# Decode attention beside a gated unit: output weights at the end of the load stream, values in 512-column products, softmax steps between transposes

## The chip, the cores and the metric

The kernel runs on one core of a Trainium2 chip. A core has TensorE (PE in the profile; its weight loads are the row PEld), VectorE (DVE), ScalarE (ACT), GpSimd (POOL), SyncE (SP) and 16 DMA engines that move data between the device memory and SBUF. TensorE writes its results to PSUM, eight banks of 128 partitions by 512 floats. The metric is the device time of one execution in microseconds (us).

## The reference

Two batch rows, one new token each, hidden size 512. The token is normalised, goes through attention over the last 4096 keys of a cache with 8 key/value heads (32 query heads, four to each kv head, head size 128), and in parallel through a gated unit with 1792 hidden columns; the input and both results are added. Everything is float32.

```python
# B, D = 2, 512; Hq, Hkv, Sk, Dh = 32, 8, 32768, 128; F = 1792
W = min(4096, max(256, Sk // 4))                        # 4096
q = (xn @ wq).reshape(B, 1, Hq, Dh).transpose(0, 2, 1, 3)
k = repeat(k_cache[:, :, Sk - W:, :], Hq // Hkv, axis=1)
v = repeat(v_cache[:, :, Sk - W:, :], Hq // Hkv, axis=1)
p = softmax(einsum("bhqd,bhkd->bhqk", q, k) * Dh ** -0.5)
a = einsum("bhqk,bhkd->bhqd", p, v).transpose(0, 2, 1, 3).reshape(B, 1, Hq * Dh) @ wo
gate, up = xn @ W_gate, xn @ W_up
h = gate * (gate > 0) * up
out = x + a + h @ W_down                                # xn = layernorm(x)
```

The inputs are 95 MB, of which the used part of both caches is 67 MB (32 heads of 2 MB: K and V, two batch rows, eight kv heads), wq and wo 8 MB each, and the three gated-unit weights 11 MB.

## The kernel before

**Loads.** All large loads go out on SP's queue, in the order in which the program uses the data: wq in four, w_gate and w_up in two each, w_down in two, then the caches head by head, then wo. They share a ring of eight buffers (`load`, line 66). A load waits until the buffer eight loads earlier has been read. x comes on ACT's queue: once on 32 partitions (`x32`, line 98, for the layer norm) and, in four small loads, spread over 128 partitions (`x4`, line 100, for the residual).

**Start.** The layer norm runs on 32 partitions; its transpose `xnT` is the stationary operand of the q, gate and up products. q is spread with zeros into `qz` (line 191), so that one product of 32 stationary columns fills the rows of one head and leaves the others unchanged. The gated unit ends in `hT`; its product with w_down (lines 226 and 227, `project`) starts the sum of the output in the PSUM tile `y_ps`.

**Attention.** The work is in four groups g = (r, b): four kv heads c of one half r of the heads, for one batch row b. For each head, `transposes` (line 234) turns 4096 x 128 keys in 32 TensorE transposes, four to a PSUM tile `pk` of 512 columns; there are four such PSUM buffers, and ACT and DVE take turns in copying them to `kT`. `scores` (line 245) multiplies `kT` with `qz` in eight products of 512 columns; four of them run on different 32-column tiles of TensorE. The scores of a whole group collect in one PSUM tile `s`: its 128 rows are (quarter of the keys q, head c, half s1, query i), its columns 512 keys.

`softmax` (line 257) is one chain over TensorE, DVE and ACT: row maxima (`m`), their transpose (`mt`), the maximum per query (`mx`, `mb`), spread back over the rows (`nm_ps`, `nm`), exponential with row sums on ACT (`p`, `l`), the transpose of the probabilities (`pp`, `pt`), and the sums per query (`lp`, `rl`). `values` (line 292) takes 32 products per head with 128 columns of V each and 4 stationary columns of `pt`, into four row quarters of `o_ps`. `finish` (line 303) copies `o_ps` once per group and, in 64 products of one column each, adds the quarters and turns the result (`op`); a multiplication with `rl` puts it into `oT`.

**Order.** The order on every engine is that of the program text (`manual_schedule`, line 63). The loop at line 329 takes, for each head c of group g, the key head of g (`kwork`: its transposes, then the scores of the head before) and the value head of g - 1. Before the first value head of a group stands the whole softmax of g - 1, after the last its `finish`. After the loop come the last softmax, the first quarter of wo, the last four value heads, the last `finish`, and the rest of wo. The projection with wo adds to `y_ps`, four products per 128 rows of wo in column tiles; the residual `x4` is added by DVE at the end (line 360), and 4 KB are stored.

Of the kernel before, what the change touches and what calls it, by code (L numbers as in the profile page):

```python
# [20 lines left out]
def kernel(  # L21
# [13 lines left out]
    P = 128  # L35
# [9 lines left out]
    # Four 128x32 column tiles of the PE run side by side: one quarter of the keys in each.  # L45
# [63 lines left out]
    # Of slot n = (c, s1), columns 32n..32n+31 hold q at 4n..4n+3 and zeros elsewhere.  # L109
# [7 lines left out]
    o_ps = ps_1.tile([P, C, P], F32, name="o_ps")  # L117
    nc.vector.memset(o_ps, 0.0)
    y_ps = ps_1.tile([P, P], F32, name="y_ps")
    nc.vector.memset(y_ps, 0.0)  # L120
# [3 lines left out]
    oT = const.tile([P, HKV, REP, B, 16], F32, name="oT")  # L124
    nc.gpsimd.memset(oT, 0.0)

    # Score rows are (q, c, s1, i): selections of them, from the identity.
    by_c = const.tile([P, C], F32, name="by_c")
    nc.vector.tensor_reduce(
        out=by_c, in_=ident.rearrange("p (q c w) -> p c q w", q=Q, c=C), op=ALU.add, axis=AX.XY  # L130
    )
    by_i = const.tile([P, REP], F32, name="by_i")
    nc.vector.tensor_reduce(
        out=by_i, in_=ident.rearrange("p (n i) -> p i n", i=REP), op=ALU.add, axis=AX.X
    )
    same_i = const.tile([P, REP, DD], F32, name="same_i")
    nc.vector.tensor_copy(same_i, by_i[:, :, None].to_broadcast([P, REP, DD]))
    sel_i = const.tile([P, REP], F32, name="sel_i")
    nc.vector.tensor_reduce(
        out=sel_i, in_=ident.rearrange("p (q w) -> p w q", q=Q)[:, 0:REP, :], op=ALU.add, axis=AX.X  # L140
    )

# [11 lines left out]
    # one Newton step on the square root: 1 / sqrt(v) = 2 / (v / s + s)  # L154
# [49 lines left out]
    dw = [load_down(h) for h in range(2)]  # L204
# [15 lines left out]
    def project(lhsT, w, start, stop):  # L220
        for e in range(Q):
            nc.tensor.matmul(  # L222
                y_ps[32 * e:32 * e + 17, :], lhsT.rearrange("p b s -> p (b s)")[:, 0:17], w[:, e * P:(e + 1) * P], start=start, stop=stop
            )

    for k in range(FB):
        project(hT[:, k], dw[k // 7][:, k % 7], k == 0, False)

# [1 line left out]
    # oT[(i, dd), kv, j, b]: head 4 kv + i, column 4 dd + j  # L230
    kts, ss, pts, rls = {}, {}, {}, {}
    turn = [0]

    def transposes(g, c, kt_in):
        kt = ktp.tile([P, W], F32, name=f"kT{g}_{c}", tag="kT")
        kts[g, c] = kt
        for s in range(W // 512):
            pk = ps_kt.tile([P, 512], F32, name=f"pk{g}_{c}_{s}", tag="kt")
            for u in range(4):
                j = 4 * s + u  # L240
                nc.tensor.transpose(pk[:, u * P:(u + 1) * P], kt_in[:, j * P:(j + 1) * P], ident)  # L241
            (nc.vector.tensor_copy if turn[0] % 2 else nc.scalar.copy)(kt[:, s * 512:(s + 1) * 512], pk)  # L242
            turn[0] += 1

    def scores(g, c):
        if c == 0:
            ss[g] = ps_1.tile([P, 512], F32, name=f"s{g}", tag="s")
        for s1 in range(S1):
            n = c * S1 + s1
            for q in range(Q):  # L250
                lo = (q * S1 + s1) * 512
                nc.tensor.matmul(  # L252
                    ss[g][32 * q:32 * q + 32, :], qz[:, g, 32 * n:32 * n + 32],
                    kts[g, c][:, lo:lo + 512], start=(n == 0), stop=(n == NSLOT - 1),
                )

    def softmax(g):
        m = work.tile([P, 1], F32, name=f"m{g}", tag="m")
        nc.vector.tensor_reduce(out=m, in_=ss[g], op=ALU.max, axis=AX.X)  # L259
        mt = ps_1.tile([1, P], F32, name=f"mt{g}", tag="misc")  # L260
# [8 lines left out]
        )  # L269
        nm_ps = ps_1.tile([P, 1], F32, name=f"nm_ps{g}", tag="misc")  # L270
# [8 lines left out]
        nc.scalar.activation(p, ss[g], AF.Exp, bias=nm, scale=SCALE, accum_out=l)  # L279
        pp = ps_1.tile([P, 4, P], F32, name=f"pp{g}", tag="misc")  # L280
        for u in range(4):
            nc.tensor.transpose(pp[:, u], p[:, u * P:(u + 1) * P], ident)  # L282
        pts[g] = work.tile([P, 4, P], F32, name=f"pt{g}", tag="pt")
        nc.vector.tensor_copy(pts[g], pp)  # L284
        lc = work.tile([P, C], F32, name=f"lc{g}", tag="lc")
        nc.vector.tensor_scalar(lc, by_c, l, None, op0=ALU.mult)
        lp = ps_1.tile([P, C], F32, name=f"lp{g}", tag="misc")
        nc.tensor.matmul(lp, same_i.rearrange("p i d -> p (i d)"), lc, start=True, stop=True)  # L288
        rls[g] = work.tile([P, C], F32, name=f"rl{g}", tag="rl")
        nc.vector.reciprocal(rls[g], lp)  # L290

    def values(g, c, v):
        for s1 in range(S1):
            for u in range(4):
                for q in range(Q):
                    lo = 32 * q + REP * (c * S1 + s1)
                    j = 4 * (q * S1 + s1) + u
                    nc.tensor.matmul(  # L298
                        o_ps[32 * q:32 * q + REP, c, :], pts[g][:, u, lo:lo + REP], v[:, j * P:(j + 1) * P],
                        start=(s1 == 0 and u == 0), stop=(s1 == S1 - 1 and u == 3),  # L300
                    )

    def finish(g):
        r, b = divmod(g, B)
        on = work.tile([P, C, P], F32, name=f"on{g}", tag="on")
        nc.scalar.copy(on, o_ps)  # L306
        ov = on.rearrange("p c (d j) -> p c j d", j=REP)
        op = ps_1.tile([P, C, REP], F32, name=f"op{g}", tag="misc")
        for c in range(C):
            for j in range(REP):  # L310
                for i in range(REP):
                    nc.tensor.matmul(  # L312
                        op[32 * i:32 * i + 32, c, j:j + 1], ov[:, c, j], sel_i[:, i:i + 1], start=True, stop=True
                    )
        nc.vector.tensor_tensor(  # L315
            oT[:, r * C:(r + 1) * C, :, b, 0], rls[g][:, :, None].to_broadcast([P, C, REP]), op, op=ALU.mult
        )
# [3 lines left out]
    def kwork(g, c, kt_in):  # L321
        transposes(g, c, kt_in)
        if pend:
            scores(*pend.pop())
        pend.append((g, c))
# [3 lines left out]
    for g in range(1, NG):  # L329
        for c in range(C):  # L330
            kt_in = load_kv(k_cache, "k", g, c)
            v_in = load_kv(v_cache, "v", g - 1, c)
            kwork(g, c, kt_in)
            if c == 0:
                softmax(g - 1)
            values(g - 1, c, v_in)
        finish(g - 1)
    scores(*pend.pop())
    g = NG - 1
    softmax(g)  # L340
    wt = load_wo(0, 2)
    vin = [load_kv(v_cache, "v", g, c) for c in range(C)]

    def project_wo(kv0, n, wt):
        for v in range(n):
            for j in range(REP):
                project(oT[:, kv0 + v, j], wt[:, v, j * D:(j + 1) * D], False, False)

    project_wo(0, 2, wt)
    for c in range(C):  # L350
        values(g, c, vin[c])
    finish(g)
    for kv in (2, 4):
        project_wo(kv, 2, load_wo(kv, 2))
    for kv, j0, j1 in ((6, 0, 4), (7, 0, 3), (7, 3, 4)):
# [34 lines left out]
```

## Time and profile before

| | us |
|---|---|
| median of 3 runs | 242.74 |
| lowest, highest | 241.59, 243.03 |
| span of the profiled execution | 239.9 |
| PE busy | 183.5 (76%) |
| PE weight loads busy | 130.7 (54%) |
| DVE busy | 62.6 (26%) |
| ACT busy | 46.9 (20%) |
| SP queue's loads, as a share of 16 DMA engines | 93.8% |

The profiled execution's own time is known by its span, from its first instruction to its last; the median of the runs is 2.84 us above that. The page divides the busy time by engine and by line. An f32 product of TensorE is recorded as two matmul records and a transpose as one, so that the 32 value products of a head stand as 64 records. The granted clock is the share of full speed that TensorE had; its mean is 0.885. The view of stages gives, for stretches of the span, the busy time of each engine with its number of instructions in brackets, the clock, the busy share of the DMA engines and the GB/s that they moved. The chain of waits follows the work that ended last back to the start: each row has its start, its length, the engine and the tile; "issue" is time in which the engine waited for nothing that the profile shows.

### The profile page before, as it was taken

What the parts mean: (1) busy time and instruction counts of PE and PEld (TensorE: products, weight loads), DVE (VectorE), ACT (ScalarE), POOL (GpSimd) and SP (SyncE); (2) the same over time, 40 slices, a digit from 0 to 9 for tenths busy, and PEclk for the clock granted to TensorE, in tenths of its full rate; (3) what the DMA queues carried; (4) which work ended last, traced back from release to release, by engine and by line L of the source; (5) the groups of instructions that cost most, each with busy time, mean ns of one, the idle gap of its engine ahead of it and who ended that gap; (6) DMA issues with size and microseconds to landing.
All of it is one profiled execution on the core that took longest, in us unless ns stands there. A gap on an engine that the chain in (4) does not pass through costs nothing.

```text
span 239.9 us, 6378 instructions
## 1 busy us (share of the span) xinstructions
PE 183.5 (76%) x2984; PEld 130.7 (54%) x2984; DVE 62.6 (26%) x122; ACT 46.9 (20%) x81; POOL 3.0 (1%) x9
## 2 busy tenths in 40 slices
PE   0194656685799949999594999989499998589464
PEld 0020111365666638777581777777277776269364
DVE  4400101102644433224043134404313440210000
ACT  2000000002433613223031123313112330100000
POOL 5000000000000000000000000000000000000000
PEclk9999788979999997999778599997769998759869
DMA  6999999999999999999999999999999999999700
GB/s 235 416 411 399 405 407 434 436 429 426 429 432 432 429 427 426 426 437 429 429 423 429 429 427 434 432 426 426 432 426 426 425 440 423 422 423 425 322 22 3
DMA packets 8030, 95.44 MB, mean 398 GB/s; under 512 B 796, under 2 KB 932, under 8 KB 2244
## 3 DMA queue, kind: packets, MB, share of 16 engines
q1 hardware_dynamic: 7820, 94.90, 93.8%
q8 instruction: 23, 0.38, 0.6%
q10 hardware_dynamic: 184, 0.13, 0.2%
q14 instruction: 3, 0.02, 0.0%
HBM read 95.03 MB, written 0.00 MB: 396 GB/s over the span
## 4 chain that ended last, share of the span: by engine, by line
PE 65%; DMA 24%; issue 4%; DVE 4%; ACT 2%; ACTq 0%
PE pk L241 25%; PE o_ps L298 14%; PE s L252 13%; DMA k<-in_A_k_cache_dram 10%; DMA wg<-in_B_W_gate_dram 7%; DMA x<-in_A_x_dram 7%; PE y_ps L222 4%; PE op L312 4%; PE pp L282 2%; ACT p L279 1%; PE g_ps L199 1%; DVE m L259 1%; DVE pt L284 1%; ACT on L306 1%; PE lp L288 1%
## 5 line engine op out<-in xcount | busy, mean ns | idle before, releaser
L241 PE MATMUL pk<-ident,k 128*128 128x128 f32 x512 | 64.8, 289 | 4.3 <-DMA k<-in_A_k_cache_dram 4.3
L241 PEld LDWEIGHTS pk<-ident,k 128*128 128x128 f32 x512 | 60.8, 150 | 10.2 <-issue 6.8
L242 DVE COPY kT<-pk 128x512 f32<-128x512 f32 x64 | 44.3, 692 | 69.9 <-PE pk L241 69.1
L242 ACT COPY kT<-pk 128x512 f32<-128x512 f32 x64 | 37.5, 586 | 97.6 <-PE pk L241 97.6
L298 PE MATMUL o_ps<-v,pt 128*4 128x128 f32 x1024 | 35.6, 299 | 2.3 <-issue 2.3
L298 PEld LDWEIGHTS o_ps<-v,pt 128*4 128x4 f32 x1024 | 29.0, 94 | 11.3 <-issue 8.2
L252 PE MATMUL s<-kT,qz 128*32 128x512 f32 x256 | 32.1, 619 | 0.0
L175 PE MATMUL q_ps<-wq,xnT 128*32 128x512 f32 x64 | 11.6, 878 | 4.9 <-DMA wq<-in_A_wq_dram 4.5
L312 PE MATMUL op<-sel_i,on 128*32 128x1 f32 x512 | 9.2, 199 | 7.2 <-issue 4.4
L252 PEld LDWEIGHTS s<-kT,qz 128*32 128x32 f32 x256 | 7.2, 112 | 12.6 <-issue 12.6
L312 PEld LDWEIGHTS op<-sel_i,on 128*32 128x32 f32 x512 | 8.6, 155 | 8.6 <-issue 4.6
L315 DVE TENSOR_TENSOR oT<-rl,op 128x16 f32<-128x16 f32 x4 | 0.7, 183 | 38.5 <-PE op L312 38.5
L222 PE MATMUL y_ps<-wo,oT 128*17 128x128 f32 x256 | 10.3, 335 | 0.0
L175 PEld LDWEIGHTS q_ps<-wq,xnT 128*32 128x32 f32 x64 | 2.4, 151 | 12.7 <-DMA wq<-in_A_wq_dram 6.4
L222 PEld LDWEIGHTS y_ps<-wo,oT 128*17 128x17 f32 x256 | 9.0, 120 | 0.6
L165 PE MATMUL xt_ps<-ident,xn 32*128 32x32 f32 x4 | 0.6, 287 | 11.3 <-DVE xn L162 11.3
L306 ACT COPY on<-o_ps 128x512 f32<-128x512 f32 x4 | 2.3, 585 | 26.7 <-PE o_ps L298 26.7
L282 PE MATMUL pp<-ident,p 128*128 128x128 f32 x16 | 3.6, 363 | 4.3 <-ACT p L279 4.3
L199 PE MATMUL g_ps<-wg,xnT 128*32 128x448 f32 x32 | 4.9, 749 | 2.5 <-DMA wg<-in_B_W_gate_dram 2.5
L165 PEld LDWEIGHTS xt_ps<-ident,xn 32*128 32x128 f32 x4 | 0.5, 208 | 11.2 <-issue 11.2
L279 ACT ACTIVATE p<-s,nm 128x512 f32<-128x512 f32 x4 | 2.7, 687 | 18.7 <-DVE nm L276 18.7
L199 PE MATMUL u_ps<-wu,xnT 128*32 128x448 f32 x32 | 3.4, 544 | 3.8 <-DMA wu<-in_B_W_up_dram 3.8
(60 smaller groups left out, 53.7 us busy)
## 6 DMA issues: line engine op xcount, KB each, us to landing
k<-in_A_k_cache_dram SPq DMA_DIRECT2D x16, 2048.0 KB, 29.7
v<-in_A_v_cache_dram SPq DMA_DIRECT2D x16, 2048.0 KB, 29.8
wq<-in_A_wq_dram SPq DMA_DIRECT2D x4, 2048.0 KB, 14.7
wo<-in_A_wo_dram SPq DMA_DIRECT2D x3, 2048.0 KB, 28.1
wg<-in_B_W_gate_dram SPq DMA_DIRECT2D x2, 1792.0 KB, 20.9
wu<-in_B_W_up_dram SPq DMA_DIRECT2D x2, 1792.0 KB
wd<-in_B_W_down_dram SPq DMA_DIRECT2D x2, 1792.0 KB, 15.2
wo<-in_A_wo_dram SPq DMA_DIRECT2D x1, 1024.0 KB
```

The source lines that it names most:

```text
L175: nc.tensor.matmul(q_ps[r][32 * c:32 * c + 32, :], xnT[:, kc, :], wqt[kc][:, n * 512:(n + 1) * 512], start=(kc == 0), stop=(kc == KC - 1),)
L199: nc.tensor.matmul(dst[32 * c:32 * c + 32, :], xnT[:, kc, :], wt[kc // 2][:, kc % 2, c * FQ:(c + 1) * FQ], start=(kc == 0), stop=(kc == KC ...
L222: nc.tensor.matmul(y_ps[32 * e:32 * e + 17, :], lhsT.rearrange("p b s -> p (b s)")[:, 0:17], w[:, e * P:(e + 1) * P], start=start, stop=stop)
L241: nc.tensor.transpose(pk[:, u * P:(u + 1) * P], kt_in[:, j * P:(j + 1) * P], ident)
L242: (nc.vector.tensor_copy if turn[0] % 2 else nc.scalar.copy)(kt[:, s * 512:(s + 1) * 512], pk)
L252: nc.tensor.matmul(ss[g][32 * q:32 * q + 32, :], qz[:, g, 32 * n:32 * n + 32], kts[g, c][:, lo:lo + 512], start=(n == 0), stop=(n == NSLOT ...
L259: nc.vector.tensor_reduce(out=m, in_=ss[g], op=ALU.max, axis=AX.X)
L279: nc.scalar.activation(p, ss[g], AF.Exp, bias=nm, scale=SCALE, accum_out=l)
L282: nc.tensor.transpose(pp[:, u], p[:, u * P:(u + 1) * P], ident)
L298: nc.tensor.matmul(o_ps[32 * q:32 * q + REP, c, :], pts[g][:, u, lo:lo + REP], v[:, j * P:(j + 1) * P], start=(s1 == 0 and u == 0), stop=( ...
L306: nc.scalar.copy(on, o_ps)
L312: nc.tensor.matmul(op[32 * i:32 * i + 32, c, j:j + 1], ov[:, c, j], sel_i[:, i:i + 1], start=True, stop=True)
```

## The change

- w_down's two loads and their projection move from before the caches to behind the last value loads; all of wo comes after them, in seven loads of 16, 16, 16, 8, 4, 2 and 2 KB per partition (before: six loads of 2, 2, 2, 1, 0.75 and 0.25 MB, the first ahead of the last value heads). The layout of wo changes with it: partition p holds 16 consecutive rows of one half (`load_wo(r, j0, j1)`).
- `values` takes 8 products per head with 512 columns of V and 16 stationary columns (four key columns u by four queries i). Of a result's 16 x 512 entries only those where u fits the column block count. ACT or DVE copies it, and `gather` picks and adds the right blocks with a stationary selection `pick`: four products of 128 columns per head, into one PSUM tile `oa` for the whole group. `finish` is a DVE multiplication; `spread_heads` brings the rows of two groups into `oT` with eight products, once per half.
- `softmax` is a generator. In the loop its steps stand between the `pk` tiles of the next group's first key head; `kT` is kept in halves of 2048 keys (three buffers instead of two full ones). The last group's softmax has no transposes beside it.
- `pk` has three PSUM buffers instead of four; `o_ps` has two tiles.
- The four loads of `x4` are gone; x is added by four products of `x32` with a selection `xsel`, which start the sum in `y_ps`.

The selections (`pick`, `by_h`, `spread`, `xsel`) are built from the identity on GpSimd and DVE ahead of the layer norm, in place of `by_c`, `by_i`, `same_i` and `sel_i`.

In the program order of TensorE, at the start of a group (here the second), before: the last transposes of key head 0, the scores of the head before it, the steps of the softmax, the first value head.

```order
L241 MATMUL pk_0_7_636<-ident,k_0_589 128x128 x4
L252 MATMUL s_462<-kT_3_532,qz 32x512 x8
L261 MATMUL mt_652<-ident,m_650 1x128
L272 MATMUL nm_ps_658<-ones,mb_656 32x1 x4
L282 MATMUL pp_668<-ident,p_665 128x128 x4
L288 MATMUL lp_677<-lc_675,same_i 128x4
L298 MATMUL o_ps<-v_0_591,pt_673 4x128 x32
```

The same place on TensorE now, from the second `pk` tile of key head 0 on:

```order
L241 MATMUL pk_0_0_1_562<-ident,k_0_545 128x128 x4
L262 MATMUL mt_568<-ident,m_560 1x128
L241 MATMUL pk_0_0_2_574<-ident,k_0_545 128x128 x4
L274 MATMUL nm_ps_580<-ones,mb_572 32x1 x4
L241 MATMUL pk_0_0_3_590<-ident,k_0_545 128x128 x4
L241 MATMUL pk_0_1_0_597<-ident,k_0_545 128x128 x4
L286 MATMUL pp_603<-ident,p_587 128x128 x4
L241 MATMUL pk_0_1_1_610<-ident,k_0_545 128x128 x4
L294 MATMUL lp_616<-l_588,by_h 16x1
L241 MATMUL pk_0_1_2_620<-ident,k_0_545 128x128 x4
L251 MATMUL s_632<-kT_0_0_553,qz 32x512 x4
L306 MATMUL o_ps_99<-v_0_547,pt_608 16x512 x8
```

One to two `pk` tiles stand between any two steps of the softmax, and the value head has 8 products instead of 32 (a second `pk` tile ahead of the scores is left out).

In the order of SP's queue, the end of the load stream before, from the last value load of the loop on:

```order
L68 DMA v_3_1846<-in_A_v_cache_dram 128x4096
L68 DMA wo_2044<-in_A_wo_dram 128x2x2048
L68 DMA v_0_2046<-in_A_v_cache_dram 128x4096
L68 DMA v_1_2048<-in_A_v_cache_dram 128x4096
L68 DMA v_2_2050<-in_A_v_cache_dram 128x4096
L68 DMA v_3_2052<-in_A_v_cache_dram 128x4096
L68 DMA wo_2282<-in_A_wo_dram 128x2x2048
L68 DMA wo_2316<-in_A_wo_dram 128x2x2048
L68 DMA wo_0_2350<-in_A_wo_dram 128x2048
L68 DMA wo_0_2368<-in_A_wo_dram 128x1536
L68 DMA wo_3_2382<-in_A_wo_dram 128x512
L361 DMA out_dram<-yo 4x2x128
```

and now, from the last group's third value load on:

```order
L69 DMA v_2_1573<-in_A_v_cache_dram 128x4096
L69 DMA v_3_1575<-in_A_v_cache_dram 128x4096
L69 DMA wd_1577<-in_B_W_down_dram 128x3584
L69 DMA wd_1579<-in_B_W_down_dram 128x3584
L69 DMA wo_0_1740<-in_A_wo_dram 128x4096
L69 DMA wo_8_1774<-in_A_wo_dram 128x4096
L69 DMA wo_0_1808<-in_A_wo_dram 128x4096
L69 DMA wo_8_1842<-in_A_wo_dram 128x2048
L69 DMA wo_12_1860<-in_A_wo_dram 128x1024
L69 DMA wo_14_1870<-in_A_wo_dram 128x512
L69 DMA wo_15_1876<-in_A_wo_dram 128x512
L416 DMA out_dram<-yo 4x2x128
```

Nine loads now stand behind the last cached value head, where there were five.

The diff, cut to its core:

```diff
-    ktp = ctx.enter_context(tc.tile_pool(name="ktp", bufs=2))
+    ktp = ctx.enter_context(tc.tile_pool(name="ktp", bufs=3))
-    ps_kt = ctx.enter_context(tc.tile_pool(name="ps_kt", bufs=4, space=PSUM))
+    ps_kt = ctx.enter_context(tc.tile_pool(name="ps_kt", bufs=3, space=PSUM))
+    ps_s = ctx.enter_context(tc.tile_pool(name="ps_s", bufs=1, space=PSUM))
...
+    def load_wo(r, j0, j1):
+        rows = NJ * P
+        src = wo[r * rows:(r + 1) * rows, :].rearrange("(p j) e -> p j e", p=P)[:, j0:j1, :]
+        return load(f"wo{r}_{j0}", src, [P, j1 - j0, D])
...
-    x4 = const.tile([P, P], F32, name="x4")
-    for e in range(Q):
-        nc.scalar.dma_start(
-            x4[32 * e:32 * e + 32, :],
-            bass.AP(tensor=x.tensor, offset=x.offset + e * P, ap=[[D, B], [0, 16], [1, P]]),
-        )
...
+    o_ps = [ps_1.tile([P, 512], F32, name=f"o_ps{k}") for k in range(2)]
...
-    dw = [load_down(h) for h in range(2)]
...
-    for k in range(FB):
-        project(hT[:, k], dw[k // 7][:, k % 7], k == 0, False)
...
+    def transposes(g, c, s1, kt_in):
+        kt = ktp.tile([P, HW], F32, name=f"kT{g}_{c}_{s1}", tag="kT")
+        kts[g, c, s1] = kt
+        for q in range(Q):
+            pk = ps_kt.tile([P, 512], F32, name=f"pk{g}_{c}_{s1}_{q}", tag="kt")
+            for u in range(4):
+                j = 4 * (4 * s1 + q) + u
+                nc.tensor.transpose(pk[:, u * P:(u + 1) * P], kt_in[:, j * P:(j + 1) * P], ident)
+            evacuate(kt[:, q * 512:(q + 1) * 512], pk)
+            yield
...
     def values(g, c, v):
+        o = o_ps[c % 2]
         for s1 in range(S1):
-            for u in range(4):
-                for q in range(Q):
-                    lo = 32 * q + REP * (c * S1 + s1)
-                    j = 4 * (q * S1 + s1) + u
-                    nc.tensor.matmul(
-                        o_ps[32 * q:32 * q + REP, c, :], pts[g][:, u, lo:lo + REP], v[:, j * P:(j + 1) * P],
-                        start=(s1 == 0 and u == 0), stop=(s1 == S1 - 1 and u == 3),
-                    )
+            for q in range(Q):
+                n = (q * C + c) * S1 + s1
+                lo = (4 * s1 + q) * 512
+                nc.tensor.matmul(
+                    o[32 * q:32 * q + 16, :], pts[g][:, n].rearrange("p u i -> p (u i)"), v[:, lo:lo + 512],
+                    start=(s1 == 0), stop=(s1 == S1 - 1),
+                )
+        ons[c] = work.tile([P, 4, P], F32, name=f"on{g}_{c}", tag="on")
+        evacuate(ons[c].rearrange("p u d -> p (u d)"), o)
...
+    def gather(g, c):
+        if c == 0:
+            oa[g] = ps_1.tile([HR, P], F32, name=f"oa{g}", tag="oa")
+        for u in range(4):
+            nc.tensor.matmul(
+                oa[g], pick[:, u, 12 - 4 * c:28 - 4 * c], ons[c][:, u],
+                start=(c == 0 and u == 0), stop=(c == C - 1 and u == 3),
+            )
...
+        nc.vector.tensor_scalar(osb[r][:, b], oa[g], rls[g], None, op0=ALU.mult)
...
+    def kwork(g, c, kt_in, others=()):
+        others = list(others)
+        for s1 in range(S1):
+            for _ in transposes(g, c, s1, kt_in):
+                if others and next(others[0], "end") == "end":
+                    others.pop(0)
+            if pend:
+                scores(*pend.pop())
+            pend.append((g, c, s1))
...
-            kwork(g, c, kt_in)
             if c == 0:
-                softmax(g - 1)
+                scores(*pend.pop())
+                kwork(g, c, kt_in, [softmax(g - 1)])
+            else:
+                kwork(g, c, kt_in)
+                gather(g - 1, c - 1)
             values(g - 1, c, v_in)
+            if c == 0 and g > 1:
+                finish_r = g - 2
+                if finish_r % B == B - 1:
+                    spread_heads(finish_r // B)
+        gather(g - 1, C - 1)
         finish(g - 1)
...
+    vin = [load_kv(v_cache, "v", g, c) for c in range(C)]
+    dw = [load_down(h) for h in range(2)]
+    for _ in softmax(g):
+        pass
...
+    for c in range(C):
+        values(g, c, vin[c])
+        if c:
+            gather(g, c - 1)
+    gather(g, C - 1)
+    finish(g)
+    for k in range(FB):
+        project(hT[:, k], dw[k // 7][:, k % 7], False)
+    spread_heads(R - 1)
+    half = NJ // 2
+    for r, j0, j1 in ((0, 0, half), (0, half, NJ), (1, 0, half), (1, half, half + 4), (1, half + 4, NJ - 2),
+                      (1, NJ - 2, NJ - 1), (1, NJ - 1, NJ)):
+        wt = load_wo(r, j0, j1)
+        for j in range(j0, j1):
+            project(oT[:, r, j], wt[:, j - j0], (r, j) == (R - 1, NJ - 1))
...
-    nc.vector.tensor_tensor(yo, x4, y_ps, op=ALU.add)
+    nc.vector.tensor_copy(yo, y_ps)
```

More of the change, by code (lines that the diff above doesn't have):

```diff
@@ L218, with evacuate @@
     nc.vector.tensor_copy(hT[:, :, :, 0], ht_ps)
-    def project(lhsT, w, start, stop):
-        for e in range(Q):
+    HW = W // S1
+    ss, pts, rls = {}, {}, {}
+    kts, osb = {}, {}
+    turn = [0]
+    def evacuate(dst, src):
+        (nc.vector.tensor_copy if turn[0] % 2 else nc.scalar.copy)(dst, src)
+        turn[0] += 1
+    def transposes(g, c, s1, kt_in):
[8 more added lines that the diff above has]
+            yield
@@ L222, in project, with scores @@
+    def scores(g, c, s1):
+        if (c, s1) == (0, 0):
+            ss[g] = ps_s.tile([P, 512], F32, name=f"s{g}", tag="s")
+        n = c * S1 + s1
+        kt = kts.pop((g, c, s1))
+        for q in range(Q):
             nc.tensor.matmul(
-                y_ps[32 * e:32 * e + 17, :], lhsT.rearrange("p b s -> p (b s)")[:, 0:17], w[:, e * P:(e + 1) * P], start=start, stop=stop
-            )
-    for k in range(FB):
-        project(hT[:, k], dw[k // 7][:, k % 7], k == 0, False)
-    kts, ss, pts, rls = {}, {}, {}, {}
@@ L232 @@
[L232 to L238, printed above, removed]
-            for u in range(4):
[L240 to L249, printed above, removed]
-            for q in range(Q):
[L251 to L255, printed above, removed]
+                ss[g][32 * q:32 * q + 32, :], qz[:, g, 32 * n:32 * n + 32],
@@ L257, in softmax @@
+                kt[:, q * 512:(q + 1) * 512], start=(n == 0), stop=(n == NSLOT - 1),
+            )
     def softmax(g):
@@ L282, in softmax @@
             nc.tensor.transpose(pp[:, u], p[:, u * P:(u + 1) * P], ident)
[L283 to L289, printed above, removed]
+        pts[g] = work.tile([P, Q * NSLOT, 4, REP], F32, name=f"pt{g}", tag="pt")
@@ L303, in finish @@
+    oa = {}
+    def gather(g, c):
[5 more added lines that the diff above has]
+                start=(c == 0 and u == 0), stop=(c == C - 1 and u == 3),
+            )
     def finish(g):
         r, b = divmod(g, B)
-        on = work.tile([P, C, P], F32, name=f"on{g}", tag="on")
-        nc.scalar.copy(on, o_ps)
-        ov = on.rearrange("p c (d j) -> p c j d", j=REP)
@@ L308, in finish @@
[L308 to L317, printed above, removed]
@@ L319, with spread_heads @@
-    pend = []
[L321 to L325, printed above, removed]
+        if b == 0:
+            osb[r] = const.tile([HR, B, P], F32, name=f"osb{r}")
+        nc.vector.tensor_scalar(osb[r][:, b], oa[g], rls[g], None, op0=ALU.mult)
+    def spread_heads(r):
+        op = ps_1.tile([P, NJ, B], F32, name=f"op{r}", tag="misc")
+        for e in range(NE):
+            nc.tensor.matmul(
+                op, spread[:, e].rearrange("h k e -> h (k e)"),
+                osb[r][:, :, e * NJ:(e + 1) * NJ].rearrange("h b j -> h j b"),
+                start=(e == 0), stop=(e == NE - 1),
+            )
+        nc.vector.tensor_copy(oT[:, r, :, :, 0], op)
@@ L327 @@
+    pend = []
+    def kwork(g, c, kt_in, others=()):
[7 more added lines that the diff above has]
+            pend.append((g, c, s1))
+        for o in others:
+            for _ in o:
+                pass
     for c in range(C):
@@ L337 @@
+        gather(g - 1, C - 1)
         finish(g - 1)
+    g = NG - 1
     scores(*pend.pop())
-    g = NG - 1
-    softmax(g)
-    wt = load_wo(0, 2)
     vin = [load_kv(v_cache, "v", g, c) for c in range(C)]
[L344 to L349, printed above, removed]
+    dw = [load_down(h) for h in range(2)]
+    for _ in softmax(g):
+        pass
@@ new lines, with project @@
+    y_ps = ps_kt.tile([P, P], F32, name="y_ps", tag="kt")
+    nc.vector.memset(y_ps, 0.0)
+    for e in range(Q):
+        nc.tensor.matmul(
+            y_ps[32 * e:32 * e + 17, :], xsel.rearrange("p b s -> p (b s)")[:, 0:17],
+            x32[:, e * P:(e + 1) * P], start=True, stop=False,
+        )
+    def project(lhsT, w, stop):
+        for e in range(Q):
+            nc.tensor.matmul(
+                y_ps[32 * e:32 * e + 17, :], lhsT.rearrange("p b s -> p (b s)")[:, 0:17],
+                w[:, e * P:(e + 1) * P], start=False, stop=stop,
+            )
```

62 lines of the change are left out of this document (32 added, 30 removed).

## The prediction

> **What bounds the kernel now.** I read the page first, for the load stream.
>
> ```profile
> span 239.9 us, 6378 instructions
> ...
> PE 183.5 (76%) x2984; PEld 130.7 (54%) x2984; DVE 62.6 (26%) x122; ACT 46.9 (20%) x81; POOL 3.0 (1%) x9
> ...
> q1 hardware_dynamic: 7820, 94.90, 93.8%
> q8 instruction: 23, 0.38, 0.6%
> q10 hardware_dynamic: 184, 0.13, 0.2%
> ...
> k<-in_A_k_cache_dram SPq DMA_DIRECT2D x16, 2048.0 KB, 29.7
> ```
>
> The loads of q1 keep the 16 DMA engines busy for 93.8% of the span; PE is busy for 76%. A cache load of 2048 KB (2.097 MB) lands 29.7 us after its issue. Then I cut the span into stages.
>
> ```profile
> core 0: us, PE busy (x) PEld busy (x) DVE busy (x) ACT busy (x) POOL busy (x), PEclk, DMA share, GB/s
> 6.00:36.00 30.00, 16.28 (x100) 4.54 (x104) 3.82 (x14) 0.88 (x2) 0.00 (x0) 0.92 1.01 408
> 36.00:42.00 6.00, 3.71 (x28) 0.69 (x20) 0.62 (x1) 0.53 (x1) 0.00 (x0) 0.82 1.03 435
> ...
> 60.00:200.00 140.00, 124.29 (x1794) 93.77 (x1792) 49.88 (x85) 40.89 (x71) 0.00 (x0) 0.90 1.01 429
> ...
> 225.00:226.00 1.00, 0.31 (x14) 0.06 (x7) 0.00 (x0) 0.58 (x1) 0.00 (x0) 0.93 0.69 289
> 226.00:227.00 1.00, 1.00 (x70) 1.00 (x72) 0.00 (x0) 0.00 (x0) 0.00 (x0) 0.50 0.59 242
> 227.00:228.00 1.00, 0.79 (x50) 0.70 (x43) 0.00 (x0) 0.00 (x0) 0.00 (x0) 0.50 0.42 164
> 228.00:229.00 1.00, 0.00 (x0) 0.00 (x0) 0.00 (x0) 0.00 (x0) 0.00 (x0) 0.50 0.24 94
> 229.00:230.00 1.00, 0.11 (x8) 0.11 (x10) 0.00 (x0) 0.00 (x0) 0.00 (x0) 0.50 0.04 14
> ```
>
> The DMA share is full in the stages up to 200 us. At 429 GB/s a cache load takes 2.097 MB / 429 GB/s = 4.89 us, so 29.7 us is a queue of six loads, and a group of eight takes 39.1 us. From 225 us the engines run out one after another; the last bytes move at about 229.3 (a share of 0.04 of 16 engines over 1 us is 0.64 engine-us: two engines for 0.3 us). Third, the chain of waits, in order of time:
>
> ```profile
> 92.04 4.00 PE pk L241 x32
> 96.04 1.85 PE s L252 x16
> 97.89 1.75 PE o_ps L298 x64
> 99.64 3.64 PE pk L241 x32
> ...
> 116.69 1.87 issue
> ...
> 126.79 0.70 DVE m L259
> ...
> 127.54 0.28 PE mt L261
> ...
> 128.48 0.27 PE nm_ps L272 x5
> ...
> 129.80 0.70 PE pp L282 x4
> ...
> 131.50 0.56 PE lp L288 x2
> 132.06 3.53 PE o_ps L298 x64
> 135.59 4.40 PE pk L241 x32
> ...
> 206.09 0.70 DVE m L259
> ...
> 211.78 3.55 PE y_ps L222 x64
> ...
> 222.07 2.35 issue
> ...
> 230.43 6.46 PE y_ps L222 x179
> 236.89 0.02 issue
> 236.91 0.29 DVE yo L360
> ```
>
> No piece here is a transfer: PE takes 135.59 - 92.04 = 43.6 us for a group that the stream delivers in 39.1. The eight ring buffers keep the stream going meanwhile, and when the last bytes are there, at 229.3, PE still owes 6.46 us of `y_ps` products. So PE's program order sets the end, 7.6 us behind a nearly full stream.
>
> **The change part by part.** *PE in a group.* An f32 product is two records (`o_ps` x64 for 32 products); a transpose is one. The new `values` has 8 products of 512 columns per head, as `scores` has: I take its 1.85 us against 1.75, no gain. `gather` adds four products per head, 8 records on a 128-column stream; the nearest row is a transpose, 3.64 / 32 = 0.114 us, so 0.91 us (0.2 us at the 1.75 / 64 of a record among four column tiles). A head costs 3.64 + 1.85 + 1.85 + 0.91 = 8.25 us, four 33.0. The softmax holds PE from 126.79 to 132.06, 5.3 us; between transposes its own PE work stays, at most 0.28 + 0.27 + 0.70 + 0.56 = 1.8 us, with some 1 to 3 us of waits for its DVE steps of 0.70 us, and the last `gather` waits about 0.7 us for an eviction. The 64 one-column `op` products go, with the 1.87 us gap among them. Together 36.5 to 38.5 us per group, under 39.1: what is late next is the load.
>
> *The tail.* Behind the last cached V come two halves of w_down (1.835 MB, 4.28 us each) and 8.39 MB of wo (19.6 us), 28.1 us of stream; the last `k`/`v` pair lands four loads earlier, 47.7 us before the stream's end. From there PE has 5.3 us to close the third group (values 1.85, two gathers, the eviction, half of a head's scores), 5.7 of softmax (206.09 to 211.78, uncovered there), 4 x (1.85 + 0.91) = 11.0 of values, and projections.
>
> ```profile
> 48.31 3.19 PE L222 MATMUL y_ps<-wd,hT 128*17 128x128 f32 x56 [0.40 <-DVE hT L218]
> ...
> 52.02 1.72 PE L222 MATMUL y_ps<-wd,hT 128*17 128x128 f32 x56 [0.52 <-DMA wd<-in_B_W_down_dram]
> ```
>
> At the faster pace, 1.72 / 56 = 0.031 us, the 112 records of w_down and 256 of wo take 11.3 us. In all 33.3 of 47.7 us: some 14.3 us of slack, so a PE that lags less than that costs nothing. The last piece, 256 KB, has 8 records: 0.25 us. At the slow pace (3.55 / 64) the pieces after the 2 MB one, which lands 4.9 us before the end, pile up: 64 + 32 + 16 + 8 + 8 records are 7.1 us, 2.2 past the last landing. Both paces stand in the rows; I take 0.5. No load waits for its buffer: the tightest is the last, which needs the first w_down half projected; that half lands 23.8 us before the end, so it is free some 20 us early. The Trainium skill (DMA: Bandwidth & Descriptors, section "Measured (HBM→SBUF, 128 partitions, SWDGE, issued from GpSimd)") speaks against the small closing loads: 1 MB alone reaches 341 GB/s, 64 KB 138. By it the last 2 MB, cut in four, would take at least 2.097 MB / 341 GB/s = 6.1 us instead of 4.9, an estimate, and the sum below would be 1.2 us more. Here pieces of 1 MB, 768 and 256 KB closed the stream before as well, queued behind others, and it fell off only from 225 us.
>
> *The stream itself.* Its bytes stay but for the four `x4` loads on ACT's queue.
>
> ```profile
> SPq L68 <- DMA x<-in_A_x_dram: 31.9, 5, 8.7
> ```
>
> SP waited 31.9 us for x loads, up to 8.7 at a time: these loads of 16 KB trickled through the first stage. In that stage the stream moved 408 GB/s, then 435 and 429. If they caused it, the gain is 30 x (1 - 408 / 429) = 1.5 us; if not, 0. The stages coincide, so I take 1.2. PE's instructions fall from 2984 product records to 1872, counted in the program. Fetches took 0.6% x 239.9 x 16 = 23 engine-us for 23 packets, 1 us of one engine each, and 37% of them go: 0.54 us averaged over the engines. The engine with the most sets the end: the shares after 225 us add up to 1.98, so equal engines would all end at 227.0 and up to 2.3 us is to be had. I take 0.7, between 0 and 1.8. Last bytes at 229.3 - 1.2 - 0.7 = 227.4, between 226.0 and 229.3.
>
> *The end.* PE sees a landing late; no row has this alone, I take 0.4 (0 to 1). Then 0.5 for the products, 0.34 from 236.89 to the issue of the output, and 2.67 to the span's end:
>
> ```profile
> 237.23 0.70 SPq L361 DMA_DIRECT2D out_dram<-yo  x1
> ```
>
> 227.4 + 0.4 + 0.5 + 0.34 + 2.67 = 231.3 us against 239.9. The median of the runs, 242.74, stands 2.84 us above this span; with that kept, **234.2 us**. The x term that moved into `y_ps` (4 products) and the added GpSimd and DVE constants lie in the first microseconds or under waits for loads: nothing, and at most 1 us of a stage in which PE is half idle.
>
> **The rivals.** *The tail runs at PE's half pace.* In the groups it would not matter: at a mean clock of 0.80 instead of 0.90 a group of 37.5 us takes 42.2, three groups lag by 9.3, under the slack. In the tail it does. For it: the granted clock is 0.50 from 226 to 230 us, and PE will wait between pieces. Against it: 0.90 over 60 to 200, and 1.72 us right after a wait for w_down. The last products end 2.2 us after landing instead of 0.5: 235.9 us. The Trainium skill (TensorE: Matmul & The Clock Gate, section "HAM oscillation — how this bites in real kernels") has it that bursts shorter than a load wait of over 3.4 us start at half clock each time. By that rule the tail with 2 us bursts each 4.9 us is a borderline case, and the trace shows both outcomes.
>
> *The stream is as long as before*: neither x4 nor the fetches count. 229.3 as last bytes, 236.1 us. For it: the coincidence is all there is.
>
> *Slower: three PSUM buffers throttle the transposes.* There were four, and now DVE steps of the softmax and evictions of `o_ps` stand among the copies.
>
> ```profile
> 57.51 0.59 ACT L242 COPY kT<-pk 128x512 f32<-128x512 f32 x1 [18.86 <-PE pk L241]
> 57.95 0.69 DVE L242 COPY kT<-pk 128x512 f32<-128x512 f32 x1 [9.69 <-PE pk L241]
> ```
>
> A buffer's round is a fill of 3.64 / 8 = 0.46, a copy of 0.69 and two handoffs of some 0.04, 1.23 us; three buffers allow 3 x 0.46 = 1.37. So it fits by 0.14 us. Each 0.1 us over it costs 32 / 3 x 0.1 = 1.1 us a group. It decides once PE's lag passes the 14.3 us of slack in three groups, at 39.1 + 4.8 = 43.9 us a group; there the gain begins to shrink, and at 43.9 + 8.6 / 3 = 46.8 it is used up, so slower beyond 47.6. At 48 us: 242.74 + 3 x 1.2 = 246 us. For that a round must take 1.37 + (48 - 37.5) / 10.7 = 2.35 us, almost twice what the rows give; in its milder form (46 to 47.6) nothing changes.
>
> **How the numbers follow.** Forecast 0.63 (232 to 235.5), half-pace tail 0.13, long stream 0.12, throttled transposes 0.12, of which 0.07 within 1% and 0.05 slower. The first three, 0.88, are all faster by over 1%, that is below 240.3 (1% is 2.4 us, about what a measurement of this kernel can tell from no change). The range goes from stream end 226.0 with quick products (226.0 + 0.4 + 0.25 + 0.34 + 2.67 + 2.84 = 232.5, less 0.5 for the runs' scatter) to both of the first rivals at once (238.0).
>
> **What would show it.** In the new profile: the chain made of DMA pieces, k and v loads waited for by `pk` and `o_ps` in each group; pairs 9.8 us apart; no softmax stretch of 5 us in the first three groups; 408 GB/s in the first stage gone to 425 or more; the last `wo` landing ahead of eight `y_ps` records and the output. Wrong it would be if PE's chain ran without a DMA piece from the first heads to the end, if groups took over 44 us, or if the DMA share fell below 0.95 between 10 and 220 us.

## The result, and the profile after

The changed kernel takes 234.77 us (median of 4 runs, 234.73 to 234.78) against 242.2 us (4 runs, 241.59 to 243.03): a ratio of 0.969, 95% interval 0.966 to 0.973. The forecast was 234.2 us, in a range of 232 to 238. Here and below a ratio leaves out runs more than 1.5% above the fastest of their kernel, while a median takes all runs.

| | before | after |
|---|---|---|
| time, median | 242.2 | 234.77 |
| span of the profiled execution | 239.9 | 233.0 |
| time above the span, same execution | not known | 1.78 (234.78) |
| last bytes of the loads (packet records of the trace) | 229.3 | 228.9 |
| last `y_ps` product | 236.9 | 229.8 |

From the page of the changed kernel, the lines that answer to those of before:

```profile
span 233.0 us, 4203 instructions
...
PE 188.5 (81%) x1872; PEld 109.5 (47%) x1872; DVE 66.5 (29%) x127; ACT 49.1 (21%) x85; POOL 5.4 (2%) x21
...
q1 hardware_dynamic: 7580, 94.90, 96.8%
q8 instruction: 14, 0.23, 0.4%
q10 hardware_dynamic: 48, 0.07, 0.1%
```

The product records are the 1872 that were counted, the fetch packets 14 instead of 23. But 96.8% of 233.0 us is 225.5 us of DMA time for the same 94.90 MB that took 93.8% of 239.9, 225.0 us. The loads' DMA time did not get shorter. The view of stages shows where:

```profile
6.00:36.00 30.00, 16.62 (x108) 4.49 (x108) 4.99 (x17) 1.41 (x3) 0.11 (x1) 0.94 1.01 421
...
60.00:200.00 140.00, 129.07 (x1091) 75.30 (x1088) 51.96 (x93) 41.17 (x72) 0.00 (x0) 0.99 1.01 426
...
225.00:226.00 1.00, 1.00 (x28) 1.00 (x21) 0.00 (x0) 0.00 (x0) 0.00 (x0) 0.50 0.97 383
226.00:227.00 1.00, 1.00 (x27) 1.00 (x20) 0.00 (x0) 0.00 (x0) 0.00 (x0) 0.50 0.54 209
227.00:228.00 1.00, 1.00 (x28) 1.00 (x23) 0.00 (x0) 0.00 (x0) 0.00 (x0) 0.50 0.40 143
228.00:229.00 1.00, 1.00 (x36) 1.00 (x32) 0.00 (x0) 0.00 (x0) 0.00 (x0) 0.81 0.26 96
```

The first stage went from 408 to 421 GB/s, but from 60 to 200 us the rate is 426 where it was 429, with the DMA engines as full as before. The chain of waits:

```profile
42.51 3.26 PE u_ps L202 x16
...
48.42 4.99 PE pk L241 x32
...
72.97 1.02 PE pk L241 x8
...
111.82 1.04 PE pk L241 x8
...
149.56 1.04 PE pk L241 x8
...
189.30 0.70 DVE m L259
...
198.25 26.02 DMA wo<-in_A_wo_dram
224.27 0.14 issue
224.40 5.44 PE y_ps L394 x128
229.84 0.02 issue
229.87 0.29 DVE yo L415
```

The groups take 38.9, 37.7 and 39.7 us, from one first `pk` to the next or to the last `m`; they took 42 to 44. That is close to the stream's pace (eight loads of 2.097 MB at 426 GB/s take 39.4 us), and PE starts the keys as soon as the gated unit lets it and holds no transfer in its chain until 198. Then the chain is the stream for 26 us. The last wo pieces come at half clock (0.50 from 225 to 228), so that the last product ends 1.0 us after the last bytes.

### The profile page after: what moved, and what is told of

Same layout as the page of the kernel before. It is cut to its first block, busy times and chain, and to the rows that moved or that the text cites. A ratio compares the mean times of both kernels' runs of the same rounds, so it can differ in the third digit from the quotient of the medians.

```text
span 233.0 us, 4203 instructions
## 1 busy us (share of the span) xinstructions
PE 188.5 (81%) x1872; PEld 109.5 (47%) x1872; DVE 66.5 (29%) x127; ACT 49.1 (21%) x85; POOL 5.4 (2%) x21
## 3 DMA queue, kind: packets, MB, share of 16 engines
q1 hardware_dynamic: 7580, 94.90, 96.8%
## 4 chain that ended last, share of the span: by engine, by line
PE 62%; DMA 29%; DVE 5%; ACT 2%; issue 1%; DVEq 0%
PE pk L241 26%; DMA wu<-in_B_W_up_dram 15%; PE s L251 14%; DMA wo<-in_A_wo_dram 11%; PE o_ps L306 11%; PE oa L321 4%; DMA x<-in_A_x_dram 3%; PE y_ps L394 2%; PE u_ps L202 1%; DVE pt L289 1%; ACT p L281 1%; PE pp L286 1%; DVE on L230 1%; DVE kT L230 1%; PE ht_ps L217 1%
## 5 line engine op out<-in xcount | busy, mean ns | idle before, releaser
L241 PE MATMUL pk<-ident,k 128*128 128x128 f32 x512 | 68.6, 282 | 0.4 <-DVE kT L230 0.4
L241 PEld LDWEIGHTS pk<-ident,k 128*128 128x128 f32 x512 | 56.2, 143 | 26.1 <-DVE kT L230 10.4
L251 PE MATMUL s<-kT,qz 128*32 128x512 f32 x256 | 34.4, 604 | 0.0
L306 PE MATMUL o_ps<-v,pt 128*16 128x512 f32 x256 | 33.7, 617 | 0.0
L321 PEld LDWEIGHTS oa<-on,pick 128*16 128x16 f32 x128 | 12.1, 97 | 14.3 <-issue 7.7
L321 PE MATMUL oa<-on,pick 128*16 128x128 f32 x128 | 16.6, 273 | 2.5 <-DVE on L230 2.5
L306 PEld LDWEIGHTS o_ps<-v,pt 128*16 128x16 f32 x256 | 10.3, 99 | 12.2 <-issue 7.2
L230 DVE COPY on<-o_ps 128x512 f32<-128x512 f32 x8 | 5.5, 692 | 31.6 <-PE o_ps L306 31.6
L202 PE MATMUL u_ps<-wu,xnT 128*32 128x448 f32 x32 | 6.4, 954 | 5.2 <-DMA wu<-in_B_W_up_dram 5.2
L230 ACT COPY on<-o_ps 128x512 f32<-128x512 f32 x8 | 4.7, 586 | 28.2 <-PE o_ps L306 28.2
```

The lines of the kernel that those rows point to most:

```text
L202: nc.tensor.matmul(dst[32 * c:32 * c + 32, :], xnT[:, kc, :], wt[kc // 2][:, kc % 2, c * FQ:(c + 1) * FQ], start=(kc == 0), stop=(kc == KC ...
L230: (nc.vector.tensor_copy if turn[0] % 2 else nc.scalar.copy)(dst, src)
L251: nc.tensor.matmul(ss[g][32 * q:32 * q + 32, :], qz[:, g, 32 * n:32 * n + 32], kt[:, q * 512:(q + 1) * 512], start=(n == 0), stop=(n == NS ...
L306: nc.tensor.matmul(o[32 * q:32 * q + 16, :], pts[g][:, n].rearrange("p u i -> p (u i)"), v[:, lo:lo + 512], start=(s1 == 0), stop=(s1 == S ...
L321: nc.tensor.matmul(oa[g], pick[:, u, 12 - 4 * c:28 - 4 * c], ons[c][:, u], start=(c == 0 and u == 0), stop=(c == C - 1 and u == 3),)
```

## The experiments

Theory A is the prediction's: once PE has caught up by the time of the last weights, the load stream sets the end, and any relief of PE will do. B has the shorter groups as the gain, C the order of the loads. The times below are compared with runs of the kernel before on the same chip.

| kernel | us | ratio (95%) | GB/s, 60 to 200 us | last bytes | last product |
|---|---|---|---|---|---|
| order alone, first | 241.04 | 0.983 (0.977 to 0.988) | | | |
| order alone, again | 239.95 | 0.982 (0.977 to 0.987) | 429 | 229.0 | 235.6 |
| changed, old order of loads | 234.77 | 0.968 (0.964 to 0.972) | 426 | 228.7 | 229.7 |
| changed, softmax whole | 239.67 | 0.987 (0.982 to 0.993) | 426 | 229.0 | 234.8 |
| changed, x4 back | 235.02 | 0.970 (0.965 to 0.974) | 426 | 229.3 | 230.3 |
| changed, buffers at 256 bytes | 232.44 | 0.958 (0.956 to 0.960) | 429 | 226.5 | 227.7 |
| changed, buffers at 64 bytes | 234.33 | 0.966 (0.964 to 0.968) | 426 | 228.5 | 229.4 |
| 256 bytes, 20 transposes as filling | 233.26 | 0.962 (0.958 to 0.965) | 429 | 226.5 | 228.3 |
| before, buffers 32 bytes off | 243.05 | one run | 425 | 231.1 | 238.2 |
| 256 bytes, values cut | 233.79 | 0.962 (0.956 to 0.968) | 429 | 227.7 | 228.6 |
| 256 bytes, x4 back | 233.96 | 0.963 (0.957 to 0.968) | 430 | 227.3 | 228.3 |
| 256 bytes, long products as filling | 232.35 | 0.956 (0.951 to 0.961) | 429 | 226.5 | 227.3 |

**The order of the loads alone.** Run twice; the view and the last three columns of the table are of the second run. The last 1 MB of wo comes in three pieces here, not two.

```diff
-    dw = [load_down(h) for h in range(2)]        # and its products, before the keys
...
+    vin = [load_kv(v_cache, "v", g, c) for c in range(C)]
+    dw = [load_down(h) for h in range(2)]
     for c in range(C):
         values(g, c, vin[c])
     finish(g)
+    for k in range(FB):
+        project(hT[:, k], dw[k // 7][:, k % 7], k == 0, False)
+    for kv in (0, 2, 4):
+        project_wo(kv, 2, load_wo(kv, 2))
...
```

> The kernel before with one thing changed: w_down and all of wo stand behind the last value loads (128-column values, whole softmax, x4 loads as before). Theory A (the load stream sets the end as soon as PE has caught up by the last weights; any relief of PE will do): keys start 8.4 us earlier (48 us instead of 56.8), groups stay at 42 to 44 us, the last softmax starts at about 198, PE reaches wo at about 221 and works through it without waiting until 229 to 231; last bytes at 229; span 233 to 235, 0.970 to 0.980 of before. Theory B (the shorter groups make the gain, the order of the loads only a part of it): PE is 10 us or more behind at the end, span 237 or more, over 0.985.

> The kernel before with w_down and wo at the end, once more, for a view that can be compared: by the first look 0.983 of before, with PE behind the stream at the end. Expected: DMA rate 429 GB/s from 60 to 200 us, groups of 42 to 44 us, the last bytes at 229, y_ps products without a wait for loads until 232 to 235, an issue gap of 2 us among them or in the last op products.

Its chain of waits, towards the end:

```profile
199.97 0.70 DVE m L255
...
218.04 1.67 PE op L308 x99
...
221.38 2.73 issue
224.12 11.51 PE y_ps L221 x342
235.62 0.02 issue
```

0.982, between A and B. The keys start 8 us earlier and the last softmax 6 (199.97 against 206.09), but the projections all lie at the end now, and PE owes 342 records at 224 us, 5 us before the last bytes. It is still PE that ends late. How much the order is worth is not pinned down: the ten runs of each measurement scatter from 236.9 to 242.2 and 243.0 us, and the medians of all of them, 241.04 and 239.95 us, are 0.994 and 0.988 of before (242.45 and 242.83) where the table's ratios are 0.983 and 0.982. By either reading it is 0.6 to 1.8%, not the whole gain of 3.1%.

**The changed kernel with the old order of the loads.**

```diff
+    dw = [load_down(h) for h in range(2)]        # before the keys, with its products
...
+    w0 = load_wo(0, 0, half)
     vin = [load_kv(v_cache, "v", g, c) for c in range(C)]
     for _ in softmax(g):
         pass
+    for j in range(half):
+        project(oT[:, 0, j], w0[:, j], False)
```

> The changed kernel with the loads in the old order: w_down ahead of the keys with its products there, the first 2 MB of wo ahead of the last four values (the PSUM tile oa shares a bank so that y_ps can have its own). Theory A: groups of 38 to 40 us as in the changed kernel, keys 8 us later, last softmax at about 198, values as they land, and after the last value 14.7 us of stream hide the rest: span 233 to 234, 0.966 to 0.973 of before. Theory C (the order of the loads makes the gain): PE ends 4 us or more behind the stream, span 237 or more, over 0.983.

0.968, and the median is the changed kernel's, 234.77 us. With PE's new code the order of the loads counts for nothing: C falls. Here the chain has keys in it; three of its rows, each as long as the transfer from its issue to its landing:

```profile
111.41 32.80 DMA k<-in_A_k_cache_dram
...
149.57 35.13 DMA k<-in_A_k_cache_dram
...
208.05 21.12 DMA wo<-in_A_wo_dram
```

PE's own idle time for them is short: 3.2 us ahead of the first key head, and 0.40 and 0.83 us at the two rows with k.

**The softmax in one piece.**

```diff
                 scores(*pend.pop())
-                kwork(g, c, kt_in, [softmax(g - 1)])
+                for _ in softmax(g - 1):
+                    pass
+                kwork(g, c, kt_in)
```

> The changed kernel with the softmax in one piece ahead of each group's first key head. Theory A: a group gets 3 to 3.5 us longer (41 to 43), so PE lags by 10 us more at the end of the third group; PE waited some 7 to 8 us for loads in the tail of the changed kernel, so 2 us or so come out: span 234 to 236, 0.973 to 0.983 of before. Rival: the interleaving is worth nothing since all of the lag is made up in the tail: 0.969 as the changed kernel. Rival: all of it comes out: 243 us of span, no gain over before.

```profile
72.39 0.70 DVE m L259
...
115.41 0.70 DVE m L259
...
156.96 0.70 DVE m L259
...
200.24 0.70 DVE m L259
...
223.28 3.68 PE y_ps L396 x127
226.96 2.46 issue
229.43 5.32 PE y_ps L396 x124
```

Groups of 43.0, 41.6 and 43.3 us; the last softmax is 10.9 us later than in the changed kernel (200.24 against 189.30), and the last product 4.9 us. So the tail took up 6 us of the lag, less than the "7 to 8", and a gap of 2.46 us among the last products, which the expectation did not have, is half of what came out. Behind the gap the clock fell to 0.50 for 3.4 us: the last 124 records took 5.32 us where the 127 ahead of the gap had taken 3.68, some 1.6 us more. The interleaving carries 4.9 us, most of the gain; the gap and the half clock behind it account for 4.1 of them. What the new `values` and `finish` carry by themselves was not run.

**The four small loads back.**

```diff
+    for e in range(Q):
+        nc.scalar.dma_start(x4[32 * e:32 * e + 32, :], ...)
-    nc.vector.tensor_copy(yo, y_ps)
+    nc.vector.tensor_tensor(yo, x4, y_ps, op=ALU.add)
```

> The changed kernel with the four small x4 loads on ACT's queue and the residual added at the end by DVE, as before. If the small loads slow the stream: the stage from 6 to 36 us falls from 421 GB/s to about 408, u_ps ends 1 us later, and the last bytes and the time come 0.5 to 1.2 us later (0.971 to 0.974 of before). If they don't (the early rate comes from how many loads are queued, or is chance): 421 GB/s and 0.969 stay.

413 GB/s in the first stage, last bytes 0.4 us later, and 0.25 us more time with overlapping intervals: an effect, smaller than forecast.

**Where the 426 comes from.** Up to here every kernel with the new constants had 426 and every one with the old 429, whatever PE did. What they share is where the eight load buffers lie, behind the constants: in the built programs at byte 35584 of a partition before, a multiple of 256, and at 41248 after, 32 past one.

```diff
+    const.tile([P, 56], F32, name="pad")        # 224 bytes; 8 floats for the 64-byte case
     x32 = const.tile([32, D], F32, name="x32")
```

> The changed kernel with 224 unused bytes per partition ahead of the constants, so that the eight load buffers start at a multiple of 256 bytes of a partition, as in the kernel before (in the changed kernel they start 32 bytes past one). If the place of the buffers costs the stream 1%: 429 GB/s instead of 426 from 60 to 200 us, last bytes 1.5 to 2.2 us earlier (226.7 to 227.4 instead of 228.9), time 232.6 to 233.3, 0.960 to 0.963 of before. If the 426 comes from the work of the engines beside the loads: 426 and 0.969 stay.

> The same with 32 unused bytes: the buffers start at a multiple of 64 bytes, 64 past a multiple of 256. If 64 bytes are what counts, as with 256 bytes: 429 GB/s, 232.6 to 233.3. If 256 bytes count, as the changed kernel: 426 GB/s, 234.8.

> The kernel before with 32 unused bytes ahead of the constants: its load buffers start 32 bytes past a multiple of 256. If the place of the buffers sets the rate: 426 GB/s instead of 429 from 60 to 200 us, while the time moves by less than 1 us since PE sets its end. If not: 429.

The stages of the kernel with 256 bytes:

```profile
6.00:36.00 30.00, 16.32 (x108) 4.65 (x108) 4.36 (x16) 0.88 (x2) 0.11 (x1) 0.93 1.01 427
...
60.00:200.00 140.00, 129.08 (x1084) 75.10 (x1085) 51.91 (x91) 41.24 (x72) 0.00 (x0) 0.98 1.01 429
...
226.00:227.00 1.00, 1.00 (x40) 0.95 (x32) 0.00 (x0) 0.00 (x0) 0.00 (x0) 0.82 0.13 51
227.00:228.00 1.00, 0.67 (x25) 0.39 (x13) 0.28 (x1) 0.00 (x0) 0.00 (x0) 1.00 0.00 0
```

and the same stage of the kernel before with its buffers 32 bytes off:

```profile
60.00:200.00 140.00, 125.05 (x1828) 94.71 (x1828) 50.19 (x85) 41.66 (x72) 0.00 (x0) 0.91 1.01 425
```

The place of the buffers sets the rate, in both kernels, and 64 bytes do not do. The packet records say the same: from 60 to 200 us a packet of 16 KB takes 613 ns in the mean wherever the buffers are at a multiple of 256 bytes, 617 or 618 where they are 32 bytes off and 616 where they are 64 off. The unused bytes move the buffers of `kT` and `work` by as much; no run moved the load buffers alone. With 256 bytes PE's work from 60 to 200 us is the same (129.08 against 129.07 us), the last bytes come 2.4 us earlier and the time falls to 232.44 us, 0.958 of before. In the kernel before, the last bytes come 1.8 us later and the one run shows 243.05 us. The Trainium skill (DMA: Bandwidth & Descriptors, section "How a descriptor splits into AXI transactions") says that a descriptor is cut at multiples of 256 bytes and that one which starts off them costs extra beats, for bytes in front of it that are fetched and not used. That is told of the side that is read; here it is the side that is written that moved, so whether it is the same thing is not shown. By the beat count of the Trainium skill's section a row of 16 KB would cost one beat in 512 more, 0.2%, an estimate; the runs show 0.7% in the rate and 1% in the stream (2.4 of 227 us).

**Fetches and x4, with the buffers in place.** The values are cut into 128 columns, with the same data and order:

```diff
-    o[32 * q:32 * q + 16, :], pts[g][:, n]..., v[:, lo:lo + 512]
+    o[32 * q:32 * q + 16, w * P:(w + 1) * P], pts[g][:, n]..., v[:, lo:lo + P]    # for w in range(4)
```

> The changed kernel with the buffers at a multiple of 256 bytes and each 512-column value product cut into four of 128 columns (same data, same stationary columns, 2640 product records instead of 1872). If the instruction fetches lengthen the stream as the prediction had it (0.7 us for 1112 records): 19 or 20 fetch packets instead of 14, last bytes 0.3 to 0.8 us later than the 226.5 of the buffers' move alone, time 232.8 to 233.4. If PE's order in the groups counts: the values take 1.75 us a head in both forms, nothing. If the fetches count for nothing: 232.4.

> The changed kernel with the buffers at a multiple of 256 bytes and the four small x4 loads back. As the prediction had it: 408 GB/s instead of 427 in the stage from 6 to 36 us, last bytes 1.2 us later (227.7), time 233.6. As the first look at x4 has it (413 against 421 GB/s, 0.4 us): last bytes 226.9, time 232.8.

From the pages of the cut kernel and of the changed one with 256 bytes, in this order:

```profile
q8 instruction: 20, 0.33, 0.5%
```

```profile
q8 instruction: 14, 0.23, 0.4%
```

Six more fetch packets, and the last bytes at 227.7 instead of 226.5 (226.5 also in the filled kernel below, measured on the same chip as this one), more than the 0.3 to 0.8 us expected. PE's busy time from 60 to 200 us stays (129.07 us), so it is not PE's time for the values. The six packets themselves took 0.93 us each, 0.35 us averaged over the 16 engines; why the last bytes moved by 1.2, the runs do not say. x4: 412 GB/s instead of 427 in the first stage and last bytes 0.7 us later, between the two expectations. The times, 233.79 and 233.96 us, stand 1.4 and 1.6 us above the filled kernel of the same chip (232.35); the runs with x4 scatter by 1.7 us.

**The tail kept busy.** Behind the products of the first two wo loads stands work into an unused PSUM tile, which leaves the result as it is: 20 transposes in the one kernel, five products of 288 columns in the other.

```diff
+            for u in range(4):                                          # five times
+                nc.tensor.transpose(fill[:, u * P:(u + 1) * P], ident, ident)
...
+            nc.tensor.matmul(fill[:, 0:288], ident, qz[:, 0], ...)      # five times
```

> The 224 bytes, and 20 transposes of the identity into an unused PSUM tile behind the products of each of the first two wo loads, so that PE is idle less between loads in the tail (they are added work and leave the result as it is). If PE's half pace on the last pieces costs what it seems to in the changed kernel (products end 1.0 us after the last bytes, 0.6 would do): granted clock 1.0 from 222 us on, 0.3 to 0.6 us less than with the 224 bytes alone. If the pace of the last products is covered by the landings: no difference.

> The buffers at a multiple of 256 bytes, and behind each of the first two wo loads five products of 288 columns into an unused PSUM tile (added work, result unchanged): 10 records of long products each instead of 20 short transposes. If the transposes lost because their instructions brought a fetch gap of 1.55 us into the last products: no such gap now, PE at full clock from 222 us on, products end 0.4 to 0.7 us earlier than with the buffers' move alone, time 231.8 to 232.1. If filling itself is of no use: 232.4 or more.

The chain's end with the transposes, and then with the long products:

```profile
224.36 1.05 PE y_ps L395 x27
225.41 1.55 issue
226.96 1.30 PE y_ps L395 x37
```

```profile
207.60 19.21 DMA wo<-in_A_wo_dram
226.81 0.04 issue
226.85 0.46 PE y_ps L395 x8
227.33 0.29 DVE yo L420
```

In both the clock is 1.00 from 222 us on. With the transposes a gap of 1.55 us appears among the last products and eats more than the clock gives. With the long products only the eight records of the last piece stand behind the stream and the products end 0.39 us earlier than without filling. The times, 232.35 and 232.44 us on two chips, can't be told apart.

## Why the prediction was right, and where it was not

- *PE's order sets the end, behind a nearly full stream.* Right. With the whole softmax, or with the order alone, PE ends 5.8 and 6.6 us after the last bytes, and the time follows PE.
- *A group of 36.5 to 38.5 us.* 38.9, 37.7 and 39.7, two of three above it: a head's piece is `pk` 1.96, `s` 0.99, `pk` 1.96, `s` 0.99, `oa` 0.74, `o_ps` 1.83, in all 8.47 us for the 8.25 of the sum, since halved scores cost 0.99 and not 0.93, and transposes 1.96 to 2.08 and not 1.82. The first group also has the load of ACT's function table, 1.28 us, in the chain, and the third the 1.90 us of `spread_heads`, for which the sum had no term.
- *What is late next is the load, in every group.* Wrong in this kernel: its chain has no transfer between 48 and 198 us. That is nearly a sign named as showing the prediction wrong (no DMA piece to the end; there is one, wo, at 198), and the k and v loads that were to show in each group are missing. PE needs 24.6 us (48.42 to 72.97) for the four key heads of the first group, 19.7 us of stream, and then runs at the stream's pace (groups of 38.8 us in the mean against 39.4), so it makes up little of that lag before the tail, where it first meets loads again. With the old order, where the keys come 8 us later, it does wait for keys, but only 0.40 and 0.83 us in the groups.
- *A slack of 14.3 us in the tail.* Too large: a lag of 10.9 us left 4.9 us over, of which 2.46 us were a gap that the sum did not have and some 1.6 the half clock behind it.
- *The stream is 1.9 us shorter (1.2 for x4, 0.7 for fetches).* The step that failed: 0.4 us. The two terms were there, mis-sized in opposite ways: x4 costs 0.7 us (0.4 with the buffers 32 bytes off), and the fetches 1.2 us for 6 packets, so by that rate 1.8 for the 9 that went. Together 2.5 at most, and with the buffers at 256 bytes the last bytes are 2.8 us earlier than before (226.5 against 229.3); the order of the loads alone had moved them by 0.3, to 229.0. What took 2.4 back was not in the sum: new constants ahead of the buffers moved them off a multiple of 256 bytes.
- *The end.* 0.4 + 0.5 us from the last bytes to the last product were 1.0. The 0.4, which no row of before had, is 0.33 where PE waits for the last piece alone (last bytes at 226.52, products from 226.85, with long products as filling). The half-pace rival was what happened: the clock was 0.50 from 225 to 228 us. It cost far less than its 2.2 us, since the products ran for 5.4 us in a row and the clock came back before the last; filling, which kept it at 1.00, gained 0.39 us. The small closing loads cost nothing: the last 2 MB in four pieces were there 4.6 us after the load ahead of them (224.27 to 228.88), not the 6.1 us of the prediction's estimate.
- *2.84 us between span and median.* Wrong by 1.1. The changed kernel's profiled execution took 234.78 us with its span of 233.0, and further runs of the kernel before 241.96 to 243.02 with spans of 240.0 to 241.2: 1.8 to 2.0 us. The profiled execution of before was one of the shorter ones.
- *Three PSUM buffers.* The rival did not come: in its chain one copy of `kT`, 0.70 us at 86.90, is all that a transpose waited for, and the groups are shorter than 43.9 us.

So the forecast of 234.2 us is right as to what sets the end, the load stream with PE caught up in the tail. That it lies within 0.6 us is in part luck, as two errors cancel: the span was forecast 1.7 us too short (231.3 against 233.0), the rest 1.1 us too long. The stream's forecast, last bytes at 227.4, lies between the 228.9 of the changed kernel and the 226.5 of the one with 256 bytes.

## What to carry to other kernels

Where PE and the load stream are nearly equal, find which of them owes work when the last bytes land; then any relief that lets PE catch up gives the same end, and a second one adds nothing (234.77 us with the loads in either order). After a change of constants, look whether the load buffers still start where they did: one row of the stages, the rate in the steady part, shows it. Short products are paid for in fetches, on a stream that is full, and, as far as these traces show, in gaps where PE runs many of them in a row.

## What the runs showed of the hardware

- Load buffers that start 32 or 64 bytes past a multiple of 256 bytes of a partition take 425 or 426 GB/s instead of 429 in steady loads of 16 KB rows, and cost 1.8 to 2.4 us of a stream of 227 to 229.
- With six more fetch packets of 16 KB the last bytes of a full stream came 1.2 us later (one kernel, one trace of each).
- Where PE runs hundreds of short products in the tail of the loads, it stops for 1.6 to 2.7 us with nothing to wait for in the profile (2.73, 2.46 and 1.55 us above). In the tail that decides: 20 transposes behind each of two loads brought such a gap, ten records of long products did not. That these gaps are fetches is argued, not tried by itself: the packet records have a fetch starting at 221.8, 226.9 and 224.5 us, beside gaps that start at 221.4, 227.0 and 225.4; but a fetch at 227.2 us in the changed kernel has no gap.
- In the changed kernel PE waited 1.1, 1.3, 1.5 and 3.1 us between the last weight loads, and the clock fell to 0.50 twice, at 214.7 us, just behind the second of these waits, and at 225.0, behind the fourth, for 3.4 us each time. The Trainium skill (TensorE: Matmul & The Clock Gate, section "HAM oscillation — how this bites in real kernels") names waits over 3.4 us; here shorter ones sufficed. Ten records of filling behind each of the first two wo loads kept the clock at 1.00 from 197 us to the end of the products.
